# An mLSTM cell with a cosine-gated block behind it: three equal cuts and the scheduler's TensorE order in place of half-height pairs and a written order

## The chip, the cores and the metric

The kernel runs on one core of a Trainium2 chip. A core has a matrix engine (TensorE, PE in the profile, with its weight loads as PEld), three engines that work element by element (VectorE or DVE, ScalarE or ACT, GpSimd or POOL), a queue engine (SyncE or SP), and DMA engines that move data between the large memory and the core's on-chip memory (SBUF). TensorE writes its results to a small accumulator memory, PSUM, which has eight banks; a bank holds 512 f32 columns over 128 partitions. Each engine works through its own list of instructions in order, and engines wait for each other only through semaphores. The metric is the time of one execution in microseconds (us) on the device; lower is better.

## The reference

Two blocks follow each other. The first is an mLSTM cell, run over 768 time steps for 4 batches and 8 heads of size 40:

```
for t in range(S):
    m_new  = max(f[t] + m, i[t])
    f_stab = exp(f[t] + m - m_new);  i_stab = exp(i[t] - m_new);  m = m_new
    C = f_stab * C + i_stab * outer(v[t], k[t])
    n = f_stab * n + i_stab * k[t]
    y[t] = sigmoid(o[t]) * (C @ q[t]) / max(|n . q[t]|, 1)
```

The second block takes each time step's 8 x 40 = 320 numbers as one row x of a matrix of 3072 rows:

```
h = x @ w_in            # 320 -> 2048
out = (h * cos(h)) @ w_out   # 2048 -> 320
```

All is computed in f32. The two weight matrices arrive as 64-bit floats, so the kernel turns their bits into 32-bit floats itself.

## The kernel before

The recurrence is not run step by step. Time is cut into 6 chunks of 128 steps (NC), and a *cell* handles one chunk of one batch, for all 8 heads at once; there are 24 cells. The state that a chunk leaves to the next is kept per batch in `st`.

The gates come first (`gate`): running sums and running maxima of the gate inputs along time give, for each chunk, the columns aT, wT, gT and the running maxima M. M of the first chunk stays on chip as M0; M of the later chunks goes to the large memory, and `load_E` brings it back, spread over 128 partitions, from POOL's queue into a tile E. For the first chunk, eight small matmuls (`pm`, L232) against one column of the identity do that spreading. `decay` then makes each head's 128 x 128 matrix of decays in E: eight DVE instructions (L233) and one exp on ACT (L235). It runs one cell ahead of its use.

A cell then takes these steps. PE transposes q and k (pt, L254), and ACT and DVE copy them out as the tiles t (L256). PE multiplies them into scores (ps, L265), 8 heads in pairs of row groups: the 40 rows of an even head start at partition 0, those of an odd head at partition 64, and the two kinds alternate. DVE multiplies scores and decays (L268). PE computes what the old state gives (pq, L274) and what the chunk itself gives (ph, L280). DVE adds the two and divides (hs, dn, y, L284 to L295), and copies y's last 64 columns once more behind its end (L296). PE transposes y (px, L304), and ACT copies it out as xT (L305). For the next chunk's state, POOL has weighted the keys (kw, L249), PE multiplies them with v (pu, L310), and DVE scales the old state (L320) and adds (L321).

The second block works on a chunk of 4 x 128 = 512 columns. The 2048 hidden features are 16 blocks of 128 (NF). `up` makes two blocks at a time: the 320 rows of w_in are cut into 128 + 128 + 64, the first two cuts are full matmuls (L335), and the 64-row rests of the two blocks are stored on partitions 0 to 63 and 64 to 127 and issued next to each other (L338), which is what y's second copy is for. `act` computes h * cos(h): two ACT passes over the result (n at L345, h at L349), a DVE instruction that takes the rounded turns away (r, written over n, L347), a sine on ACT (L350), and a product on POOL (g, L352). `down` multiplies g with w_out (po, L366) and adds up over the 16 blocks; the four batches have a PSUM bank each, so all four sums grow together, and after the last block ACT copies each out (L369) and SP stores it.

PSUM is divided into 2 banks for the cells (ps_a), 2 for up (ps_u) and 4 for down (ps_o). The four cells of the first chunk run before any up, with the cells taking turns between ps_a and ps_o. After them PE's order is written out by hand (`manual_schedule`): an up pair, a step of the cell of the next chunk, a down of the pair before, the next step, and so on. The order on the other engines, and PE's before that point, is made by a scheduler that plans with estimated times and priorities.

w_in is converted in 10 pieces beside the first four cells, w_out in 16 pieces beside the first chunk's ups. One piece is a DMA from SP's queue into a tile `bits`, two ACT instructions, three on DVE (L124, L126, L128) and an add on POOL (L129); five bits buffers are in use. q, k and v have five buffer sets.

Of the kernel before, what the change touches and what calls it, by code (L numbers as in the profile page):

```python
# [11 lines left out]
FP = mybir.dt.float32  # L12
I32 = mybir.dt.int32
# [15 lines left out]
def kernel(  # L29
# [32 lines left out]

    NK = DM // 128
    KL = NK * 128
    assert DM - KL == 64 and NF % 2 == 0
    NB = 5
# [5 lines left out]
    p4 = ctx.enter_context(tc.tile_pool(name="p4", bufs=4))  # L72
    pb = ctx.enter_context(tc.tile_pool(name="pb", bufs=5))
    dram = ctx.enter_context(tc.tile_pool(name="dram", bufs=1, space=bass.MemoryType.DRAM))
    ps_a = ctx.enter_context(tc.tile_pool(name="ps_a", bufs=2, space=bass.MemoryType.PSUM))
    ps_u = ctx.enter_context(tc.tile_pool(name="ps_u", bufs=2, space=bass.MemoryType.PSUM))
    ps_o = ctx.enter_context(tc.tile_pool(name="ps_o", bufs=4, space=bass.MemoryType.PSUM))
# [23 lines left out]

    w_in_sb = wp.tile([128, NK, DFF], FP, name="w_in_sb")

    w_in_l = wp.tile([128, NF // 2, 128], FP, name="w_in_l")
# [6 lines left out]
    def to_float32(dst, src):  # L111
        rows, n = dst.shape
        r = slice(0, rows)
        bits = pb.tile([128, WP, 2], I32, name="bits", tag="bits")
        for part, piece in src:
            nc.sync.dma_start(out=bits[part, 0:n], in_=piece)
# [14 lines left out]
    def weights_in(f):  # L131
        for i in range(NK):
            to_float32(w_in_sb[:, i, ts(f, WP)], [(slice(0, 128), w_in_bits[ts(i, 128), ts(f, WP)])])

    def weights_in_l(f):
        src = w_in_bits[KL:DM].rearrange("r (a e n) two -> r e a n two", e=2, n=128)
        n = WP // 128
        to_float32(w_in_l[:, ts(f, n)].rearrange("p a n -> p (a n)"),
                   [(slice(64 * e, 64 * e + 64), src[:, e, ts(f, n)]) for e in range(2)])

    def weights_out(f):
        to_float32(w_out_sb[:, f], [(slice(0, 128), w_out_bits[ts(f, 128)])])
# [20 lines left out]
    def gate(c):  # L163
# [13 lines left out]
        pg = ps_o.tile([128, 4, BH], FP, name="pg", tag="o")  # L177
# [14 lines left out]
    gp = ctx.enter_context(tc.tile_pool(name="gp", bufs=8))  # L192
# [19 lines left out]
    def load_E(n):  # L212
        c, b = divmod(n, B)
        E = p4.tile([128, H, C], FP, name="E", tag="E")
        if c > 0:
            src = M_d[b * H:(b + 1) * H, ts(c - 1, C)]
            nc.gpsimd.dma_start(out=E, in_=src.unsqueeze(0).to_broadcast([128, H, C]))  # L217
        loaded[n] = E

    def decay(n):  # L220

        c, b = divmod(n, B)
        E = loaded[n]
        for h in range(H):
            g = b * H + h
            m = E[:, h]
            if c == 0:

                if h % HP == 0:
                    pm = ps_u.tile([128, HP, C], FP, name="pm", tag="up")  # L230
                m = pm[:, h % HP]
                nc.tensor.matmul(m, ident[0:BH, g:g + 1].to_broadcast([BH, 128]), M0, start=True, stop=True)  # L232
            nc.vector.scalar_tensor_tensor(out=E[:, h], in0=m, scalar=aT[:, c, g:g + 1],  # L233
                                           in1=late, op0=OP.subtract, op1=OP.max)
        nc.scalar.activation(out=E, in_=E, func=AF.Exp, scale=-1.0)  # L235

    def cell(n, psum, tag):

# [8 lines left out]
        if c < NC - 1:  # L247
            kw = p2.tile([128, H, 64], FP, name="kw", tag="kw")
            nc.gpsimd.tensor_tensor(out=kw, in0=ks[i], in1=cols(wT, 64), op=OP.mult)  # L249
        tT = []  # L250
        for src, copy in ((qs[i], nc.scalar.copy), (ks[i], nc.vector.tensor_copy)):
            pt = psum.tile([128, HP, C], FP, name="pt", tag=tag)
            for p in range(HP):
                nc.tensor.transpose(pt[:, p], src[:, 2 * p:2 * p + 2].rearrange("p j d -> p (j d)"), ident)  # L254
            t = p2.tile([128, HP, C], FP, name=f"t{len(tT)}", tag=f"t{len(tT)}")
            copy(out=t, in_=pt)  # L256
            tT.append(t)
        qT, kT = tT
        yield

        ps = [psum.tile([128, HP, C], FP, name="ps", tag=tag) for _ in range(2)]
        for p in range(HP):
            for j in range(2):
                r = slice(64 * j, 64 * j + D)
                nc.tensor.matmul(ps[j][:, p], kT[r, p], qT[r, p], start=True, stop=True)  # L265
        for j in range(2):
            w = E.rearrange("p (a j) t -> p a j t", j=2)[:, :, j]
            nc.vector.tensor_tensor(out=w, in0=ps[j], in1=w, op=OP.mult)  # L268
        yield

        if c > 0:
            pq = psum.tile([128, H, D1], FP, name="pq", tag=tag)
# [3 lines left out]
        ph = psum.tile([128, H, D1], FP, name="ph", tag=tag)  # L276
        for j in range(2):
            for p in range(HP):
                h = 2 * p + j
                nc.tensor.matmul(ph[:, h], E[:, h], vs[i][:, h], start=True, stop=True)  # L280
        hs = ph
        if c > 0:
# [9 lines left out]
        y = p2.tile([128, 2 * DM - KL], FP, name="y", tag="y")  # L292
        yh = y[:, 0:DM].rearrange("p (h d) -> p h d", h=H)
        nc.vector.tensor_tensor(out=yh, in0=sig[c][:, b], in1=hs[:, :, 0:D], op=OP.mult)
        nc.vector.tensor_tensor(out=yh, in0=yh, in1=dn.unsqueeze(2).to_broadcast([128, H, D]), op=OP.mult)  # L295
        nc.vector.tensor_copy(out=y[:, DM:], in_=y[:, KL:DM])  # L296
        yield


        if b == 0:  # L300
            xT[c] = p2.tile([128, NK + 1, B, C], FP, name="xT", tag="xT")
        px = psum.tile([128, NK + 1, C], FP, name="px", tag=tag)
        for i2 in range(NK + 1):
            nc.tensor.transpose(px[:, i2], y[:, ts(i2, 128)], ident)  # L304
        nc.scalar.copy(out=xT[c][:, :, b], in_=px)  # L305

        if c < NC - 1:
            pu = psum.tile([128, HP, 2, D1], FP, name="pu", tag=tag)
# [13 lines left out]
        yield  # L322
# [4 lines left out]
    def up(c, f2):  # L327
        pair = [ps_u.tile([128, B * C], FP, name="pup", tag="up") for _ in range(2)]

        def x(i, r=slice(0, 128)):  # L330
            return xT[c][r, i].rearrange("p b t -> p (b t)")

        for e, pu in enumerate(pair):
            for i in range(NK):
                nc.tensor.matmul(pu, w_in_sb[:, i, ts(2 * f2 + e, 128)], x(i), start=(i == 0), stop=False)  # L335
        for e, pu in enumerate(pair):
            r = slice(64 * e, 64 * e + 64)
            nc.tensor.matmul(pu, w_in_l[r, f2], x(NK, r), start=False, stop=True)  # L338
        for e, pu in enumerate(pair):
            act(c, 2 * f2 + e, pu)  # L340

    def act(c, f, pu):

        n = p3.tile([128, B * C], I32, name="n", tag="n")
        nc.scalar.activation(out=n, in_=pu, func=AF.Copy, bias=0.25)  # L345
        r = n.bitcast(FP)
        nc.vector.scalar_tensor_tensor(out=r, in0=pu, scalar=0.25, in1=n, op0=OP.add, op1=OP.subtract)  # L347
        h = p3.tile([128, B * C], FP, name="h", tag="h")
        nc.scalar.activation(out=h, in_=pu, func=AF.Copy, scale=TWO_PI)  # L349
# [5 lines left out]
    po = {}  # L355

    def down(c, f2):
        if f2 == 0:
            po[c] = [ps_o.tile([128, DM], FP, name="po", tag="o") for _ in range(B)]
        last = f2 == NF // 2 - 1  # L360

        order = [(f, b) for f in (2 * f2, 2 * f2 + 1) for b in range(B)]
        if last:
            order.sort(key=lambda fb: fb[1])
        for f, b in order:
            nc.tensor.matmul(po[c][b], gs[c, f][:, ts(b, C)], w_out_sb[:, f], start=(f == 0), stop=(f == NF - 1))  # L366
            if f == NF - 1:
                o = p2.tile([128, DM], FP, name="o_sb", tag="o_sb")
                nc.scalar.copy(out=o, in_=po[c][b])  # L369
                nc.sync.dma_start(out=out[b * S + c * C:b * S + (c + 1) * C], in_=o)  # L370


    N = NC * B

    def ahead(n):

        if n + NB - 1 < N:
            load(n + NB - 1)
        if n + 3 < N:
            load_E(n + 3)  # L380
        if n % B == B - 1 and n + 1 < N:
            gate_o(n // B + 1)

    gates_in()
    load(0)
    for n in range(3):
        load_E(n)
    gate(0)
    for n in range(1, NB - 1):
        load(n)  # L390
    gate_o(0)


    for n in range(B):
        decay(n)
        for _ in cell(n, *((ps_a, "a"), (ps_o, "o"))[n % 2]):
            pass
        ahead(n)
# [4 lines left out]
        weights_in(n)  # L403
        if n % 2 == 1:
            weights_in_l(n // 2)
    decay(B)

    with tc.manual_schedule(engines={mybir.EngineType.PE}):  # L410
        for c in range(NC):
            for b in range(B):
                n = (c + 1) * B + b
                steps = iter(())
                if n < N:
                    steps = cell(n, ps_a, "a")
# [46 lines left out]
```

## Time and profile before

| | |
|---|---|
| median of 3 runs | 684.95 us (684.32 to 685.29) |
| the profiled execution's own time | 685.29 us |
| its span in the profile | 683.5 us |
| mean granted TensorE clock | 0.985 of full speed |
| PE busy | 627.3 us, 2786 records |
| DVE, ACT, POOL busy | 349.4, 305.7, 193.5 us |
| moved by DMA | 41.42 MB, most of it in packets under 512 bytes |

A profile shows one execution. Its groups collect the instructions of one line, engine and shape: busy time, mean length of one, and the idle time of the engine just before them with what ended it. Starts and lengths of single instructions are in its timeline; matmuls overlap in a pipeline, so what a matmul costs is read from the distance between starts, not from its length. The span can be cut into stages, and each engine's busy time read per stage.

### The profile page before, as it was taken

How to read it: one execution, taken by the hardware profiler on the slowest of the kernel's cores; microseconds unless marked ns; L12 is line 12 of the kernel's file. 1: busy time of each engine (PE TensorE's matmuls, PEld its weight loads, DVE VectorE, ACT ScalarE, POOL GpSimd, SP SyncE). 2: the span in 40 equal slices, each digit the busy share in tenths (PEclk: the TensorE clock that was granted, in tenths of full speed). 3: DMA queues.
4: the chain of work that ended last, by engine and by line, in shares of the span. 5: the costliest groups of instructions: out<-in, count | busy, mean ns of one | idle time of the engine just before them, and what ended most of it. 6: DMA issues, size and time to landing. Idle time of an engine off the chain costs nothing.

```text
span 683.5 us, 7830 instructions
## 1 busy us (share of the span) xinstructions
PE 627.3 (92%) x2786; PEld 395.6 (58%) x2786; DVE 349.4 (51%) x752; ACT 305.7 (45%) x498; POOL 193.5 (28%) x190
## 2 busy tenths in 40 slices
PE   4998559969999999999999999999999999999997
PEld 3887535545565565566556556556556566655554
DVE  5467788782663663663573573563563343321110
ACT  2433557744537525527435437434435232334332
POOL 4023245451331331331321321322222212122221
PEclk9999988979999999999999999999999999999999
DMA  9966856511223211223311232211111000000001
GB/s 141 200 121 122 211 145 146 126 41 20 60 57 80 61 34 26 60 62 76 61 41 20 59 72 67 60 42 20 40 32 39 0 1 0 1 24 16 0 1 38
DMA packets 110888, 41.42 MB, mean 61 GB/s; under 512 B 101041, under 2 KB 105137, under 8 KB 110849
## 3 DMA queue, kind: packets, MB, share of 16 engines
q1 hardware_dynamic: 107888, 30.25, 23.0%
q0 software_dynamic: 2912, 10.57, 4.9%
q8 instruction: 22, 0.36, 0.2%
q14 instruction: 18, 0.14, 0.1%
q10 hardware_dynamic: 48, 0.10, 0.0%
HBM read 36.90 MB, written 4.01 MB: 60 GB/s over the span
## 4 chain that ended last, share of the span: by engine, by line
PE 65%; DVE 21%; ACT 9%; issue 3%; DMA 1%; POOLq 0%; POOL 0%; DVEq 0%; ACTq 0%
PE pup L335 24%; PE po L366 11%; PE pup L338 7%; PE ph L280 7%; DVE st L320 7%; PE ps L265 4%; PE pq L274 3%; PE pu L310 3%; ACT L350 2%; ACT h L349 2%; ACT n L350 2%; DVE E L233 2%; PE px L304 2%; DVE n L347 2%; PE pm L232 2%
## 5 line engine op out<-in xcount | busy, mean ns | idle before, releaser
L366 PE MATMUL po<-w_out_sb,g 128*128 128x320 f32 x768 | 217.2, 436 | 0.2 <-POOL g L352 0.2
L352 POOL TENSOR_TENSOR g<-h,n 128x512 f32<-128x512 f32 x96 | 121.2, 1286 | 245.8 <-ACT n L350 239.0
L335 PE MATMUL pup<-xT,w_in_sb 128*128 128x512 f32 x384 | 181.1, 616 | 0.6 <-ACT xT L305 0.6
L366 PEld LDWEIGHTS po<-w_out_sb,g 128*128 128x128 f32 x768 | 142.2, 190 | 59.9 <-issue 6.1
L347 DVE SCALAR_TENSOR_TENSOR n<-pup,n 128x512 f32<-128x512 f32 x96 | 62.1, 686 | 208.2 <-ACT n L345 208.2
L345 ACT ACTIVATE n<-pup 128x512 int32<-128x512 f32 x96 | 52.3, 593 | 173.1 <-PE pup L338 173.1
L335 PEld LDWEIGHTS pup<-xT,w_in_sb 128*128 128x128 f32 x384 | 71.9, 196 | 76.7 <-issue 71.5
L268 DVE TENSOR_TENSOR E<-ps,E 128x512 f32<-128x512 f32 x48 | 30.9, 685 | 71.3 <-PE ps L265 71.2
L349 ACT ACTIVATE h<-pup 128x512 f32<-128x512 f32 x96 | 56.8, 592 | 11.1 <-DVE n L347 11.1
L233 DVE SCALAR_TENSOR_TENSOR E<-E,aT,late 128x128 f32<-128x128 f32 x160 | 60.7, 440 | 0.1
L350 ACT ACTIVATE n<-n 128x512 f32<-128x512 f32 x96 | 60.1, 626 | 0.2
L305 ACT COPY xT<-px 128x384 f32<-128x384 f32 x24 | 11.5, 478 | 107.6 <-PE px L304 107.6
L217 POOL DMA_DIRECT2D E<-M_d x20 | 18.4, 922 | 138.1 <-ACT h L349 67.5
L280 PE MATMUL ph<-vs,E 128*128 128x41 f32 x384 | 53.0, 302 | 2.4 <-DVE E L268 2.4
L338 PE MATMUL pup<-xT,w_in_l 64*128 64x512 f32 x192 | 54.2, 641 | 0.0
L280 PEld LDWEIGHTS ph<-vs,E 128*128 128x128 f32 x384 | 51.6, 215 | 3.2 <-DVE E L268 2.9
L320 DVE TENSOR_TENSOR st<-st,dec 64x164 f32<-64x164 f32 x32 | 49.3, 1541 | 0.5
L265 PE MATMUL ps<-t,t 40*128 40x128 f32 x384 | 34.0, 319 | 9.6 <-DVE t L256 7.6
L265 PEld LDWEIGHTS ps<-t,t 40*128 40x128 f32 x384 | 28.1, 215 | 20.4 <-ACT t L256 8.1
L304 PE MATMUL px<-ident,y 128*128 128x128 f32 x72 | 15.2, 313 | 26.2 <-DVE y L295 25.1
L249 POOL TENSOR_TENSOR kw<-ks,wT 128x512 f32<-128x512 f32 x20 | 21.0, 1050 | 62.1 <-issue 56.1
L338 PEld LDWEIGHTS pup<-xT,w_in_l 64*128 64x128 f32 x192 | 14.5, 184 | 36.4 <-issue 36.4
(75 smaller groups left out, 561.1 us busy)
## 6 DMA issues: line engine op xcount, KB each, us to landing
E<-M_d POOLq DMA_DIRECT2D x20, 512.0 KB, 4.8
bits<-in_moe_w_out_dram SPq DMA_DIRECT2D x16, 320.0 KB, 3.3
bits<-in_moe_w_in_dram SPq DMA_DIRECT2D x8, 512.0 KB, 5.0
qs<-in_q_dram SPq DMA_DIRECT2D x24, 160.0 KB, 3.3
ks<-in_k_dram SPq DMA_DIRECT2D x24, 160.0 KB, 3.6
vs<-in_v_dram SPq DMA_DIRECT2D x24, 160.0 KB, 2.8
o<-in_o_gate_dram SPq DMA_DIRECT2D x24, 160.0 KB, 3.7
out_dram<-o_sb SPq DMA_DIRECT2D x24, 160.0 KB, 1.8
```

Source lines behind the costliest of these rows:

```text
L233: nc.vector.scalar_tensor_tensor(out=E[:, h], in0=m, scalar=aT[:, c, g:g + 1], in1=late, op0=OP.subtract, op1=OP.max)
L265: nc.tensor.matmul(ps[j][:, p], kT[r, p], qT[r, p], start=True, stop=True)
L280: nc.tensor.matmul(ph[:, h], E[:, h], vs[i][:, h], start=True, stop=True)
L320: nc.vector.tensor_tensor(out=s, in0=s, in1=d.unsqueeze(2).to_broadcast([64, HP, D1]), op=OP.mult)
L335: nc.tensor.matmul(pu, w_in_sb[:, i, ts(2 * f2 + e, 128)], x(i), start=(i == 0), stop=False)
L338: nc.tensor.matmul(pu, w_in_l[r, f2], x(NK, r), start=False, stop=True)
L345: nc.scalar.activation(out=n, in_=pu, func=AF.Copy, bias=0.25)
L347: nc.vector.scalar_tensor_tensor(out=r, in0=pu, scalar=0.25, in1=n, op0=OP.add, op1=OP.subtract)
L349: nc.scalar.activation(out=h, in_=pu, func=AF.Copy, scale=TWO_PI)
L350: nc.scalar.activation(out=r, in_=r, func=AF.Sin, scale=TWO_PI_DOWN)
L352: nc.gpsimd.tensor_tensor(out=g, in0=h, in1=r, op=OP.mult)
L366: nc.tensor.matmul(po[c][b], gs[c, f][:, ts(b, C)], w_out_sb[:, f], start=(f == 0), stop=(f == NF - 1))
```

## The change

The other kernel does the same computation with these differences.

- **Cuts.** The 320 rows are cut at head borders into 120, 120 and 80, all from partition 0. `up` makes one block of 128 features at a time with three matmuls; there are no half-height pairs, y is written over the sigmoid tile, and xT is copied out by two ACT copies. w_in has 12 pieces.
- **Scores.** The four even heads go first into a bank of their own, then the four odd heads into another.
- **Order.** The order by hand is gone; the scheduler places all of PE's work. The cell is one function without steps, with the decays inside it, the weighted keys (kw) behind y, and pq behind ph. `down` takes one batch at a time over all 16 blocks, after the chunk's ups in the source.
- **Buffers.** PSUM: 3 banks for the cells, 2 for the scores, 2 for up, 1 for down. 19 buffers for g (8 before), 3 for E (4), 3 for bits (5), 4 sets for q, k and v (5). E is loaded two cells ahead (three before).
- **Early stage.** w_in's pieces are issued ahead of each of the first four cells; the cells use the same three banks.

```diff
-    NK = DM // 128
-    KL = NK * 128
-    NB = 5
+    KH = 3
+    cuts = [(h * D, min(h + KH, H) * D) for h in range(0, H, KH)]
+    KD = KH * D
+    full = DM // KD
+    NK = len(cuts)
+    NB = 4
...
-    p4 = ctx.enter_context(tc.tile_pool(name="p4", bufs=4))
-    pb = ctx.enter_context(tc.tile_pool(name="pb", bufs=5))
-    ps_a = ctx.enter_context(tc.tile_pool(name="ps_a", bufs=2, space=bass.MemoryType.PSUM))
+    ps_a = ctx.enter_context(tc.tile_pool(name="ps_a", bufs=3, space=bass.MemoryType.PSUM))
+    ps_s = ctx.enter_context(tc.tile_pool(name="ps_s", bufs=1, space=bass.MemoryType.PSUM))
...
-    ps_o = ctx.enter_context(tc.tile_pool(name="ps_o", bufs=4, space=bass.MemoryType.PSUM))
+    ps_o = ctx.enter_context(tc.tile_pool(name="ps_o", bufs=1, space=bass.MemoryType.PSUM))
...
-        bits = pb.tile([128, WP, 2], I32, name="bits", tag="bits")
+        bits = p3.tile([128, WP, 2], I32, name="bits", tag="bits")
...
     def weights_in(f):
-        for i in range(NK):
-            to_float32(w_in_sb[:, i, ts(f, WP)], [(slice(0, 128), w_in_bits[ts(i, 128), ts(f, WP)])])
+        for i, (lo, hi) in enumerate(cuts):
+            to_float32(w_in_sb[0:hi - lo, i, ts(f, WP)], w_in_bits[lo:hi, ts(f, WP)], nc.sync)
...
-    gp = ctx.enter_context(tc.tile_pool(name="gp", bufs=8))
+    gp = ctx.enter_context(tc.tile_pool(name="gp", bufs=19))
...
-        E = p4.tile([128, H, C], FP, name="E", tag="E")
+        E = p3.tile([128, H, C], FP, name="E", tag="E")
...
-        ps = [psum.tile([128, HP, C], FP, name="ps", tag=tag) for _ in range(2)]
-        for p in range(HP):
-            for j in range(2):
-                r = slice(64 * j, 64 * j + D)
-                nc.tensor.matmul(ps[j][:, p], kT[r, p], qT[r, p], start=True, stop=True)
         for j in range(2):
+            r = slice(64 * j, 64 * j + D)
+            ps = ps_s.tile([128, HP, C], FP, name=f"ps{j}", tag=f"s{j}")
+            for p in range(HP):
+                nc.tensor.matmul(ps[:, p], kT[r, p], qT[r, p], start=True, stop=True)
...
-        y = p2.tile([128, 2 * DM - KL], FP, name="y", tag="y")
...
-        nc.vector.tensor_copy(out=y[:, DM:], in_=y[:, KL:DM])
+        y = sig[c][:, b]
...
         if c < NC - 1:
+            kw = p2.tile([128, H, 64], FP, name="kw", tag="kw")
+            nc.gpsimd.tensor_tensor(out=kw, in0=ks[i], in1=cols(wT, 64), op=OP.mult)
...
-    def up(c, f2):
-        pair = [ps_u.tile([128, B * C], FP, name="pup", tag="up") for _ in range(2)]
...
-        for e, pu in enumerate(pair):
-            for i in range(NK):
-                nc.tensor.matmul(pu, w_in_sb[:, i, ts(2 * f2 + e, 128)], x(i), start=(i == 0), stop=False)
-        for e, pu in enumerate(pair):
-            r = slice(64 * e, 64 * e + 64)
-            nc.tensor.matmul(pu, w_in_l[r, f2], x(NK, r), start=False, stop=True)
...
+    def up(c, f):
+        pu = ps_u.tile([128, B * C], FP, name="pup", tag="up")
+        for i, (lo, hi) in enumerate(cuts):
+            r = slice(0, hi - lo)
+            nc.tensor.matmul(pu, w_in_sb[r, i, ts(f, 128)], xT[c][r, i].rearrange("p b t -> p (b t)"),
+                             start=(i == 0), stop=(i == NK - 1))
...
+    def down(c, b):
+        po = ps_o.tile([128, DM], FP, name="po", tag="o")
+        for f in range(NF):
+            nc.tensor.matmul(po, gs[c, f][:, ts(b, C)], w_out_sb[:, f], start=(f == 0), stop=(f == NF - 1))
+        o = p2.tile([128, DM], FP, name="o_sb", tag="o_sb")
+        nc.scalar.copy(out=o, in_=po)
+        nc.sync.dma_start(out=out[b * S + c * C:b * S + (c + 1) * C], in_=o)
...
-    with tc.manual_schedule(engines={mybir.EngineType.PE}):
...
+    for c in range(NC):
+        for b in range(B):
+            for f in range(b * NF // B, (b + 1) * NF // B):
+                up(c, f)
+                if c == 0:
+                    weights_out(f)
+            if c + 1 < NC:
+                step((c + 1) * B + b)
+        for b in range(B):
+            down(c, b)
```

## The prediction

> **What bounds the kernel now.** I read the page's busy table and chain first, then a table of six stages of my own cut (one for each chunk of 128 time steps), then the groups that the change touches, and at last the timeline of single instructions, because a group's mean hides how matmuls overlap.
>
> ```profile
> PE 627.3 (92%) x2786; PEld 395.6 (58%) x2786; DVE 349.4 (51%) x752; ACT 305.7 (45%) x498; POOL 193.5 (28%) x190
> ...
> PE 65%; DVE 21%; ACT 9%; issue 3%; DMA 1%; POOLq 0%; POOL 0%; DVEq 0%; ACTq 0%
> ...
> L335 PE MATMUL pup<-xT,w_in_sb 128*128 128x512 f32 x384 | 181.1, 616 | 0.6 <-ACT xT L305 0.6
> L338 PE MATMUL pup<-xT,w_in_l 64*128 64x512 f32 x192 | 54.2, 641 | 0.0
> L265 PE MATMUL ps<-t,t 40*128 40x128 f32 x384 | 34.0, 319 | 9.6 <-DVE t L256 7.6
> L304 PE MATMUL px<-ident,y 128*128 128x128 f32 x72 | 15.2, 313 | 26.2 <-DVE y L295 25.1
> ```
>
> TensorE (PE) is the bound: 92% busy, and its idle time has one large cause, px waiting for y (25.1 us). The stages, whose columns are length, then busy time of PE, its weight loads, DVE, ACT and POOL, the granted clock and DMA, say where PE is full. The first line starts at the first up pair, the second at the second pair:
>
> ```profile
> 85.90:102.56 16.66, 9.56 (x38) 5.06 (x37) 15.23 (x30) 9.54 (x17) 8.15 (x8) 0.81 0.58 142
> 102.56:203.62 101.06, 90.80 (x411) 56.27 (x409) 68.19 (x139) 53.87 (x91) 38.41 (x36) 0.93 0.32 74
> 203.62:305.72 102.10, 97.03 (x462) 60.21 (x462) 55.75 (x109) 48.22 (x75) 27.84 (x24) 1.00 0.25 53
> 509.70:603.04 93.34, 92.60 (x430) 56.77 (x428) 35.04 (x66) 34.37 (x63) 21.25 (x16) 1.00 0.02 8
> 603.04:683.50 80.46, 76.81 (x240) 41.11 (x240) 10.31 (x16) 28.85 (x56) 19.97 (x16) 1.00 0.05 17
> ```
>
> In a steady chunk (third line) PE idles 5.1 of 102.1 us, so PE work that is added there is paid nearly in full. Prices come from starts in PE's timeline and, for y's wait, from DVE and POOL beside it (columns: start, length):
>
> ```profile
> 589.11 1.16 PE L265 MATMUL ps<-t,t 40*128 40x128 f32 x16
> 590.20 3.70 PE L335 MATMUL pup<-xT,w_in_sb 128*128 128x512 f32 x8
> ...
> 612.14 3.60 PE L335 MATMUL pup<-xT,w_in_sb 128*128 128x512 f32 x8
> 615.66 1.13 PE L338 MATMUL pup<-xT,w_in_l 64*128 64x512 f32 x4
> 616.72 4.57 PE L366 MATMUL po<-w_out_sb,g 128*128 128x320 f32 x16
> ...
> 350.12 3.38 DVE L320 TENSOR_TENSOR st<-st,dec 64x164 f32<-64x164 f32 x1
> 374.67 0.31 DVE L320 TENSOR_TENSOR st<-st,dec 64x164 f32<-64x164 f32 x1
> ...
> 350.80 2.50 POOL L352 TENSOR_TENSOR g<-h,n 128x512 f32<-128x512 f32 x2
> ...
> 355.08 0.52 PE L304 MATMUL px<-ident,y 128*128 128x128 f32 x3 [1.14 <-DVE y L295]
> ```
>
> Every f32 matmul shows as two records, or passes. Eight 512-column passes take 615.66 - 612.14 = 3.52, 0.44 each. Four half-height passes take 616.72 - 615.66 = 1.06, not 4 x 0.44 = 1.76: the halves on rows 0-63 and 64-127 overlap.
>
> **The change, part by part.**
>
> *Up projection.* A pair of feature blocks costs 3.52 + 1.06 = 4.58 now. Afterwards each block has three cuts of 120, 120 and 80 rows, all starting at row 0, so nothing is paired: 12 passes of 0.44 = 5.28. 48 pairs x 0.70 = +33.6 us, on PE. Bounds: passes of 128 and 64 rows have the same mean (616 and 641 ns), so fewer rows buy nothing; that the 80-row cut scales with its rows (80/128) would take 96 x 0.88 x 0.375 = 31.7 off. I take +33.6.
> The Trainium skill (TensorEngine Tiling, Theoretical Speedup) puts two-way row tiling at up to 2x. By that the pair of halves would be 0.88, and the loss 0.88 per pair, 42 us; the row above gives 1.06 and 33.6, and the measurement decides.
>
> *Scores (ps).* Now the two row groups alternate, 16 passes in 590.20 - 589.11 = 1.09. Afterwards four products of one group precede four of the other. Neighbours that do not pair: ph, 16 passes in 1.75 (595.84 to 597.59 in the same timeline), and pt, four passes in 0.49, so 1.96 for 16. I take 1.80, nearest to ph, for +0.71; ends +0.66 and +0.87, and 0 if order did not matter. Twenty cells after the first up: +14.2.
>
> *Order and waits.* The fixed order px, up pair, pt, po, ps, up pair, pq, ph, po goes; the scheduler's order of the built program has, in each steady cell, ps, one ph, pq, half of pu, the other ph, half of pu, three up matmuls, px, eight up matmuls, pt, three po, one up. Before px, PE now has half of pu (0.43) and three ups (3 x 0.88 = 2.64) after ph, 3.1 us. On DVE from ph to y: hs add 0.42, two state adds 0.65, then dn, y, dn, reciprocal, y 1.44 (353.53 to 354.97), 2.5 in all; the state decays now stand ahead of the hs add, beside ph. So y is just covered. In the steady chunks PE idles 5.07, 4.67, 5.09 and 0.74 us now (stage length less busy), 15.6 in all; I leave it about 1 us a chunk and take -11. Lower end: all gone, -15.6. Upper end: the decay on DVE took 3.38 while POOL worked through an E issue and two g products and 0.31 when it did not; if a block of up to 3.1 lands between ph and y in each of 16 cells, PE pays 3.1 - 0.6 = 2.5 a cell, +40.
> The Trainium skill (SBUF — State Buffer, shared port pair) calls this an exclusive lock held for a whole instruction, with the loser fully blocked. The 3.38 against 0.31 agrees; since the new order spreads the g products singly instead of two together, the rule lets a block recur at more places, which speaks against the change and for the upper end.
> kw moves after y in the source, but POOL still issues it cells ahead of pu; nobody waits. The decays of E move into the cell: PE does not wait for them while po and pt (2.6 us) stand before ps. E is fetched two cells ahead instead of three, from POOL's queue, and lands in 4.8 us against a cell of about 19; covered twice over. q, k, v come four cells ahead into four buffers behind out stores on SP; a whole chunk of slack. The dropped y copy (L296, 236 ns on DVE) and a second xT copy on ACT are off the path, and 19 g buffers in place of 8 hold a chunk's 16 blocks and three of the next.
>
> *Down projection.* Same 384 matmuls, 0.55 each (616.72 to 621.13 is 4.41 for eight). With one PSUM bank, each of the 24 sums must be copied out before the next starts. The nearest row is the up pair at 603.04, which waited 0.57 for ACT to copy xT out; the copy of a sum is no longer (0.428 against 0.478 mean). In the new order one up matmul (0.88) covers that gap within five chunks; only in the last one three gaps are bare: 3 x 0.6 = +1.8. If the fifteen covers fail, 9 more.
>
> *Up to the second up pair (102.56 us now).* Weight pieces go from 10 to 12 (L129 on POOL 1.31 each, DVE 1.85 a piece by L124, L126, L128). PE takes the first four cells strictly one after another, where two of them interleave now. PE is not the limit here (9.56 of the last 16.66). Each cell is a chain at PE's early pace (from its timeline there): pt 1.9, eight decays and exp 3.5, unpaired scores about 4, two products 1.3, ph and pu 5.5, y 2, px and its copy 1, together 19, and 2 of DVE's weight work between. The first ends near 32, since sigmoid now ends at 31.4 on ACT; three more make 95; of the first ups the seventh matmul needs the first block's r, which DVE reaches after some 9 us of weights and decays: I get 105 for the same progress. +3, between -8 (interleaving hidden anyway) and +25 (three bits buffers instead of five make SP's queue hold loads behind weights).
> *First chunk.* 10.3 idle now, DVE at 68 of 101. w_out's 16 pieces stay in it or just before: 0, between -8 and +12.
>
> **Sum.** 33.6 + 14.2 - 11 + 1.8 + 3 = +41.6. The profiled execution took 685.29 with a span of 683.5, 1.8 outside; 683.5 + 41.6 + 1.8 = 726.9. The median of the runs, 684.95, lies 0.3 lower: 727.
>
> **Rivals.**
> *DVE's chain becomes the wait (slower still).* POOL's blocks fall between ph and y in all 16 cells: +40 instead of -11, 778; in half of them, 758. For it: 3.38 in nearly every cell now, and 6.51 us of wait for y at 141.9 in the first chunk. Against: the decays stand earlier in the new order.
> *The stage before the ups grows.* +25 instead of +3: 749. For it: fewer buffers and one cell at a time at a granted clock of 0.81. Against: PE has slack.
> *Not slower: the early stage speeds up.* PE is busy 75 of the first 102.56 us (sum over 17-us windows), much of it slowly: ps takes 2.0 there, 1.09 later. If the new order ran it densely at full speed, that work is near 45 us. It decides if the second pair starts before 102.6 - 38.6 = 64 us; at 58 the time would be 727 - 47.6 = 679. Against: PE there waits for DVE, whose own work there is 66 us now (same windows) and does not shrink.
> *The order does not matter to ps, and waits vanish wholly.* 0 instead of 14.2 and -15.6: 708.
>
> **How the numbers follow.** My sum within 15 us (712 to 742): 52%. DVE's chain: 20% (742 to 780). Early stage longer: 13% (735 to 760). Waits vanish: 10% (698 to 712). Faster: 4%; within 0.2%, about what a measurement of this kernel can tell: 1%; slower 95%. The range 702 to 762 leaves out the faster case, the bottom of the fourth and the top of the second, some 15%.
>
> **What would show it.** Up: 576 records, PE start to start 0.44, no pairs. ps: near 1.8 for 16 passes. px's wait for y: a few us in all; if it is 30 or more, DVE's chain was the step that failed. po's wait for the copy only in the last three sums. The first up near 96 us, the steady chunk near 105. A ps that still takes 1.1, or a first up before 70, would make the forecast wrong.

## The result, and the profile after

| | before | after |
|---|---|---|
| median of 4 runs each | 684.92 us (684.32 to 685.29) | 747.72 us (745.29 to 750.87) |
| ratio | | 1.092, 95% interval 1.0866 to 1.0975 |
| the profiled execution, its span | 685.29 us, 683.5 us | 745.29 us, 743.4 us |

The change costs 62.8 us; 42 were forecast. The time lies in the predicted range, 20.7 us above the number. Below, `after_raw` and `after_three` are given without one execution each that was over 1.5% above the fastest of its kernel. The same views as before, now of the changed kernel: the page's busy table, chain and the groups of up, scores and px.

```profile
PE 675.4 (91%) x2786; PEld 435.7 (59%) x2786; DVE 321.0 (43%) x734; ACT 317.7 (43%) x529; POOL 196.1 (26%) x189
...
PE 69%; DVE 13%; DMA 10%; issue 3%; SPq 2%; ACT 2%; POOL 0%; ACTq 0%; DVEq 0%; POOLq 0%
...
L310 PE MATMUL pup<-xT,w_in_sb 120*128 120x512 f32 (+1 forms) x576 | 271.2, 611 | 10.5 <-DVE n L318 10.5
L239 DVE SCALAR_TENSOR_TENSOR E<-E,aT,late 128x128 f32<-128x128 f32 x160 | 62.8, 451 | 23.5 <-DMA E<-M_d 23.4
L247 PE MATMUL ps<-t,t 40*128 40x128 f32 x384 | 50.1, 313 | 0.4 <-ACT t L226 0.3
L297 PE MATMUL px<-ident,o 128*120 128x128 f32 (+1 forms) x72 | 14.1, 311 | 21.0 <-DVE o L271 19.3
```

PE stays the bound. Two things are new: up (L310) now waits for r on DVE (L318), and DVE's decays (L239) wait 23.4 us for the DMA that brings E. px still waits 21.0 us in all (26.2 before), although only a few us of it were to stay. The chain holds 10% DMA; it held 1%.

The stages of the changed kernel, with the same columns as before (length, busy PE, PEld, DVE, ACT, POOL, granted clock, DMA share, GB/s). The second line shown starts where the third block of 128 features begins, the same progress as the second pair before:

```profile
0.00:106.12 106.12, 73.56 (x300) 62.23 (x301) 68.15 (x195) 41.63 (x73) 32.98 (x50) 1.00 0.75 134
...
113.43:225.77 112.34, 102.71 (x447) 64.78 (x447) 62.48 (x132) 59.81 (x96) 36.41 (x33) 0.98 0.31 68
225.77:337.47 111.70, 104.98 (x463) 66.55 (x462) 50.04 (x105) 51.87 (x82) 29.52 (x25) 1.00 0.23 49
...
557.37:664.40 107.03, 104.67 (x429) 65.84 (x428) 30.00 (x64) 35.92 (x67) 21.20 (x17) 0.95 0.04 12
664.40:743.40 79.00, 74.12 (x219) 40.92 (x217) 10.37 (x15) 27.85 (x50) 19.01 (x15) 1.00 0.03 11
```

The difference of the spans, 743.4 - 683.5 = 59.9, splits without a rest. The same progress is reached at 113.43 instead of 102.56: +10.9. From there to the end it is 629.97 instead of 580.94 us: PE's busy time grew by 43.1 and its idle time by 5.9 (35.4 against 29.5). The clock is no part of this difference: behind that point the kernel before had 0.93 over 101.06 us, the changed one 0.98 over 112.34 and 0.95 over 107.03, some 7 us of full clock lost in each. A steady chunk takes 111.70 us (102.10 before), with PE idle for 6.7.

### The profile page after: what moved, and what is told of

Its sections match the earlier page's. It is cut to its first block, busy times and chain, and to the rows that moved or that the text cites. A ratio compares the mean times of both kernels' runs of the same rounds, so it can differ in the third digit from the quotient of the medians.

```text
span 743.4 us, 7889 instructions
## 1 busy us (share of the span) xinstructions
PE 675.4 (91%) x2786; PEld 435.7 (59%) x2786; DVE 321.0 (43%) x734; ACT 317.7 (43%) x529; POOL 196.1 (26%) x189
## 4 chain that ended last, share of the span: by engine, by line
PE 69%; DVE 13%; DMA 10%; issue 3%; SPq 2%; ACT 2%; POOL 0%; ACTq 0%; DVEq 0%; POOLq 0%
PE po L327 27%; PE pup L310 22%; DMA E<-M_d 8%; PE ph L253 7%; DVE E L239 5%; PE ps L247 4%; PE pt L224 3%; PE pq L258 2%; PE pu L278 2%; DVE E L249 2%; DMA bits<-in_moe_w_in_dram 2%; SPq L201 2%; PE pm L238 1%; DVE n L318 1%; PE px L297 1%
## 5 line engine op out<-in xcount | busy, mean ns | idle before, releaser
L310 PE MATMUL pup<-xT,w_in_sb 120*128 120x512 f32 (+1 forms) x576 | 271.2, 611 | 10.5 <-DVE n L318 10.5
L310 PEld LDWEIGHTS pup<-xT,w_in_sb 120*128 120x128 f32 (+1 forms) x576 | 106.5, 194 | 128.3 <-issue 95.4
L318 DVE SCALAR_TENSOR_TENSOR n<-pup,n 128x512 f32<-128x512 f32 x96 | 65.0, 686 | 211.0 <-ACT h L316 210.5
L239 DVE SCALAR_TENSOR_TENSOR E<-E,aT,late 128x128 f32<-128x128 f32 x160 | 62.8, 451 | 23.5 <-DMA E<-M_d 23.4
L329 ACT COPY o_sb<-po 128x320 f32<-128x320 f32 x24 | 10.2, 425 | 138.5 <-PE po L327 121.7
L247 PEld LDWEIGHTS ps<-t,t 40*128 40x128 f32 x384 | 42.9, 209 | 17.0 <-ACT n L319 5.9
L247 PE MATMUL ps<-t,t 40*128 40x128 f32 x384 | 50.1, 313 | 0.4 <-ACT t L226 0.3
L226 DVE COPY t<-pt 128x512 f32<-128x512 f32 x24 | 16.6, 690 | 44.7 <-PE pt L224 44.4
L241 ACT ACTIVATE E<-E 128x1024 f32<-128x1024 f32 x24 | 25.3, 1055 | 21.9 <-DVE E L239 21.9
L297 PE MATMUL px<-ident,o 128*120 128x128 f32 (+1 forms) x72 | 14.1, 311 | 21.0 <-DVE o L271 19.3
L118 ACT ACTIVATE wm<-bits 128x320 int32<-128x320 uint32 (+2 forms) x28 | 15.9, 566 | 37.5 <-POOL w_in_sb L126 15.5
L298 ACT COPY xT<-px 120x256 f32<-120x256 f32 x24 | 8.8, 367 | 49.1 <-PE px L297 49.0
```

What stands on the lines that cost most here:

```text
L247: nc.tensor.matmul(ps[:, p], kT[r, p], qT[r, p], start=True, stop=True)
L310: nc.tensor.matmul(pu, w_in_sb[r, i, ts(f, 128)], xT[c][r, i].rearrange("p b t -> p (b t)"), start=(i == 0), stop=(i == NK - 1))
```

## The experiments

Seven kernels start from the changed one and undo one thing (or three), five start from the kernel before and do one thing. Ratios are to the kernel before, which was run again beside each. The changed kernel was not; its 747.72 stands for it, and `after_gp17`, which differs from it by two buffers, had 747.70.

### Steady chunks: is it E's landing that holds up DVE's queue?

The timeline of one steady cell of the changed kernel (columns: start, length, and in brackets the idle time before it):

```profile
373.37 0.49 DVE L262 TENSOR_TENSOR hs<-hs,ph 128x328 f32<-128x328 f32 x1 [0.89 <-PE ph L253]
373.63 0.92 POOL L208 DMA_DIRECT2D E<-M_d  x1 [3.44 <-PE ph L253]
374.09 1.57 DVE L266 TENSOR_SCALAR dn<-hs 128x8 f32<-128x8 f32 x1
374.58 1.06 POOL L275 TENSOR_TENSOR kw<-ks,wT 128x512 f32<-128x512 f32 x1
377.41 0.52 PE L297 MATMUL px<-ident,o 128*120 128x128 f32 x3 [0.97 <-DVE o L271]
378.63 3.20 DVE L239 SCALAR_TENSOR_TENSOR E<-E,aT,late 128x128 f32<-128x128 f32 x8 [0.64 <-DMA E<-M_d]
381.75 0.68 DVE L318 SCALAR_TENSOR_TENSOR n<-pup,n 128x512 f32<-128x512 f32 x1
382.48 2.84 PE L310 MATMUL pup<-xT,w_in_sb 120*128 120x512 f32 x6 [0.26 <-DVE n L318]
```

With three E buffers, POOL can refill one only when ph has read it (373.63, after a wait of 3.44 for ph). The scheduler puts the eight decays on that fresh E at once into DVE's list. DVE works in order, so it stands until the DMA lands at 378.63, takes 3.20 for the decays, and only then makes r (L318), for which up waits. The same POOL burst starts right behind ph and falls on dn, which takes 1.57 instead of 0.16: px waits 0.97.

`after_raw` takes the reason for the wait away: the DMA fills a tile of its own, of two buffers, and the decays go from it into E. To make room, g has 17 buffers; `after_gp17` has that alone.

```diff
+            raw = p2.tile([128, H, C], FP, name="Mb", tag="Mb")
-            nc.gpsimd.dma_start(out=E, in_=src...)
+            nc.gpsimd.dma_start(out=raw, in_=src...)
...
+        E = p2.tile([128, H, C], FP, name="E", tag="E")
-            m = E[:, h]
+            m = raw[:, h] if c > 0 else None
```

> The changed kernel with the spread maxima read into a tile of their own (2 buffers) and the decays written into E (2 buffers); g has 17 buffers instead of 19 to make room. So the load's buffer is freed by the decays and no longer by ph of a cell. Theory: in the changed kernel the load waits for ph, then the decays sit in DVE's queue waiting for the load to land, ahead of r, and POOL's issue of the load beside kw holds up the dn instruction; so px's wait for y (0.97 in most cells) and up's wait for r (0.26 to 1.16) shrink by 12 to 20 us, to 728 to 736. Rival: the waits come from the g products and the length of DVE's chain whatever the load does: 747 within 4.

> The changed kernel with 17 buffers for g instead of 19, as a control for the run with the load's own tile. Both theories: 747 within 4, since 16 hold a chunk and only the first block of the next chunk is made during the sums of the last.

`after_raw`: 738.69 us (728.91 to 738.84), ratio 1.0736 (1.0661 to 1.0811). `after_gp17`: 747.70 us, ratio 1.0905 (1.0865 to 1.0945), the same as the changed kernel. The median fell by 9, between the two expectations. The times of `after_raw` follow the granted clock: 728.91 us at 0.991, 738.84 in the profiled execution at 0.972, and the changed kernel's 745.29 us also came at 0.991, so at like clock it is 16. Two whole chunks each, from one first score to the next, show it without the clock's part (first the changed kernel, then `after_raw`):

```profile
236.29:347.12 110.83, 104.12 (x460) 66.20 (x461) 49.45 (x105) 49.14 (x78) 28.43 (x25) 1.00 0.22 48
347.12:457.65 110.53, 104.13 (x461) 66.22 (x461) 48.77 (x105) 49.14 (x78) 28.41 (x24) 1.00 0.23 49
```

```profile
251.41:357.35 105.94, 103.98 (x462) 66.88 (x462) 43.42 (x105) 50.13 (x79) 28.56 (x25) 1.00 0.25 51
357.35:463.27 105.92, 103.11 (x460) 65.85 (x459) 43.11 (x104) 48.77 (x78) 28.44 (x25) 1.00 0.23 50
```

PE's busy time stays within 1 us, and its idle time falls from 6.6 to 2.4 a chunk. In the trace the up group's wait for r falls from 10.5 to 1.7 us, px's for DVE from 19.3 to 12.8. In the second of the two chunks px's waits were 3.84 us and up's 1.62; `after_raw` has 1.23 and none. So the run shows that these waits hang on when E's buffer comes free, at 4.8 us a chunk. It changes three things at once and doesn't part them: the decays wait for no DMA, r moves in among them, and POOL issues the load later, away from dn, which takes 0.92 in place of 1.57. Why its clock was lower (0.81 to 0.86 between 107 and 230 us) is not shown.

Up's wait for r does not need the landing, as `after_ps_alt` (under Scores) shows, where E's buffers are those of the changed kernel:

```profile
349.92 3.21 DVE L239 SCALAR_TENSOR_TENSOR E<-E,aT,late 128x128 f32<-128x128 f32 x8 [0.17 <-DMA E<-M_d]
353.05 0.68 DVE L320 SCALAR_TENSOR_TENSOR n<-pup,n 128x512 f32<-128x512 f32 x1
353.79 2.84 PE L312 MATMUL pup<-xT,w_in_sb 120*128 120x512 f32 x6 [1.14 <-DVE n L320]
```

The decays wait only 7.3 us for the DMA in that run, but up waits 14.1 for r: eight decays of 3.2 us ahead of r in DVE's list are enough.

### Up: what are the unpaired cuts worth?

`before_up_split` does what the change does to the pairs: each block's 64-row rest follows its own two cuts.

```diff
         for e, pu in enumerate(pair):
             for i in range(NK):
                 nc.tensor.matmul(pu, w_in_sb[:, i, ts(2 * f2 + e, 128)], x(i), start=(i == 0), stop=False)
-        for e, pu in enumerate(pair):
             r = slice(64 * e, 64 * e + 64)
```

> The kernel before with one edit: each feature block's 64-row matmul follows its own two full ones, so the two halves of a pair are no longer neighbours; nothing else moves. If the half-height pair's overlap is what the three equal cuts give up, the time rises by 48 x 0.70 = 33.6 us to about 718 (715 to 721). If TensorE's idle time absorbs it (29.5 us idle after the second pair), the rise stays below 10, at most 695. In the profile the 64-row passes would go from a start distance of 0.27 on average to 0.44.

715.30 us (714.99 to 715.70), ratio 1.0441 (1.0424 to 1.0458): +30.3, as the theory had it, but not for its reason. From its PE timeline in the last chunk:

```profile
634.10 1.88 PE L335 MATMUL pup<-xT,w_in_sb 128*128 128x512 f32 x4
635.91 1.12 PE L337 MATMUL pup<-xT,w_in_l 64*128 64x512 f32 x2
636.97 1.98 PE L335 MATMUL pup<-xT,w_in_sb 128*128 128x512 f32 x4
638.88 1.12 PE L337 MATMUL pup<-xT,w_in_l 64*128 64x512 f32 x2
639.93 4.57 PE L365 MATMUL po<-w_out_sb,g 128*128 128x320 f32 x16
```

A lone half-height rest takes 1.06 us for two passes (636.97 - 635.91), as much as two paired rests take for four, and more than two full passes (0.88). A pair is 639.93 - 634.10 = 5.83, 1.25 more than before, which is 60 us over 48 pairs. PE's busy time did grow by 55 (682.4 against 627.3), and its idle time fell by 25 (31.3 against 56.2): the slower up covers y, and px's wait fell from 26.2 to 4.9. The run therefore doesn't price the changed kernel's cuts. Their price is read in the changed kernel itself, where 90 passes of 120 and 80 rows run on end:

```profile
664.40 38.86 PE L310 MATMUL pup<-xT,w_in_sb 120*128 120x512 f32 x90
703.10 8.78 PE L327 MATMUL po<-w_out_sb,g 128*128 128x320 f32 x32
712.39 8.88 PE L327 MATMUL po<-w_out_sb,g 128*128 128x320 f32 x32 [0.52 <-ACT o_sb L329]
```

(703.10 - 664.40) / 90 = 0.43 a pass, 5.16 for a pair's 12 passes against 4.58: +0.58 to +0.70 a pair, 28 to 34 us. The 80-row cut is no cheaper (604 ns mean against 614).

`after_pair` gives the changed kernel the old cuts and pairs back:

```diff
-    def up(c, f):
-        pu = ps_u.tile([128, B * C], FP, name="pup", tag="up")
+    def up(c, f2):
+        pair = [ps_u.tile([128, B * C], FP, name="pup", tag="up") for _ in range(2)]
...
+        for e, pu in enumerate(pair):
+            r = slice(64 * e, 64 * e + 64)
+            nc.tensor.matmul(pu, w_in_l[r, f2], x(NK, r), start=False, stop=True)
```

> The changed kernel with the old cuts of the up projection alone (128, 128 and 64 rows, the two 64-row halves of a pair next to each other, on rows 0-63 and 64-127). Theory (the unpaired cuts cost PE 48 x 0.6 to 0.7 us, and nothing else takes it up): 747.7 - 29 to 34, so 714 to 719 us, with a pair at 4.6 in the trace. Rival (PE's longer work covered waits, as when the halves were separated in the kernel before: PE's busy time grew by 55 us there, its idle time fell by 25, and the time by 30 only): px and the up projection wait longer for DVE here, more than 15 us is given back, and the time is 730 or more.

803.59 us (801.47 to 805.25), ratio 1.173 (1.1703 to 1.1758): 56 us slower, where the theory had 29 to 34 faster. The rival holds, far beyond what it named. From its PE timeline:

```profile
392.96 0.70 PE L340 MATMUL po<-w_out_sb,g 128*128 128x320 f32 x2
396.08 5.40 PE L318 MATMUL pup<-xT,w_in_sb 128*128 128x512 f32 x8 [2.41 <-DVE n L331]
401.40 1.13 PE L321 MATMUL pup<-xT,w_in_l 64*128 64x512 f32 x4
```

A pair takes both banks of up at once, and the next pair needs both free; in this order only pt and one po stand between these two pairs (392.03 to 393.66), so PE waits for ACT and DVE to empty them (30.3 us before up, 22.2 before ph). E's landing has a part in it: DVE's decays wait 48.1 us for the DMA here (23.4 in the changed kernel), and in this cell r came behind them:

```profile
393.76 1.66 DVE L244 SCALAR_TENSOR_TENSOR E<-E,aT,late 128x128 f32<-128x128 f32 x6 [3.33 <-DMA E<-M_d]
395.34 0.68 DVE L331 SCALAR_TENSOR_TENSOR n<-pup,n 128x512 f32<-128x512 f32 x1
```

And the pause costs twice: the eight passes behind it take 401.40 - 396.08 = 5.32, not 3.52, at a granted clock of 0.68. The mean clock is 0.917 over 800.9 us, up to 66 us of full clock lost against 7 in the changed kernel; by this estimate it is the larger part of the loss. PE's idle time is 26 us longer. The Trainium skill (TensorE: Matmul & The Clock Gate, What's actually happening) says that PE's clock is throttled by default and only sustained activity releases it; the rows agree in kind. So the old cuts alone are no remedy in this order. That pairs need the written order, with a block of po between two pairs, is argued and not shown: no run has pairs with a tile of its own for the load.

### Scores

`before_ps_grouped` and `after_ps_alt` swap the two loops, in the kernel before (even heads first; its diff is shown) and in the changed one (alternating again).

```diff
-        for p in range(HP):
-            for j in range(2):
+        for j in range(2):
+            for p in range(HP):
                 r = slice(64 * j, 64 * j + D)
                 nc.tensor.matmul(ps[j][:, p], kT[r, p], qT[r, p], start=True, stop=True)
```

> The kernel before with one edit: the four even heads' scores are issued first, then the four odd ones. Theory: neighbours in different row groups overlap, grouped ones don't; the changed kernel's trace has 1.68 us for 16 grouped passes against 1.09 alternating, so 20 to 24 cells x 0.59 = +12 to +14 us, 697 to 699. Rival: the order of the scores does not reach the end, since DVE's product or the waits after it set the pace: 685 within 2.

> The changed kernel with the score products alternating between the two row groups again, all else as it is. Theory: 16 passes take 1.1 instead of 1.7 to 1.8 us, 16 cells in the steady part and 4 early: 747.7 - 10 to 14, so 733 to 738 us. Rival (the scores stand where PE has slack, or DVE's products of the first group start later and take it back): 744 us or more.

`before_ps_grouped`: 702.81 us (702.58 to 703.11), ratio 1.026 (1.0244 to 1.0275), +17.8. The two parts of its time:

```profile
0.00:91.66 91.66, 71.69 (x294) 60.33 (x295) 52.30 (x172) 31.38 (x49) 23.15 (x44) 1.00 0.81 149
91.66:700.80 609.14, 570.83 (x2493) 350.78 (x2492) 296.13 (x580) 273.70 (x450) 169.52 (x146) 0.99 0.19 46
```

Behind the first up it is 609.14 instead of 597.60: +11.5, or 0.58 for each of the 20 cells there, where 0.71 was forecast; the scores themselves take 1.64 instead of 1.09. The rest is the early stage, +5.8, where the first cell's scores alone take 3.02 instead of 2.01. The rival falls; the theory, +12 to +14 in all, counted the early cells no dearer than the others.

`after_ps_alt`: 724.88 us (723.51 to 727.26), ratio 1.0594 (1.0566 to 1.0623): 22.8 gained, beyond both expectations. ps accounts for 14.3 (the group falls from 50.1 to 35.8). PE's idle time is 5.8 lower: the scheduler now puts four up matmuls ahead of px in most steady cells instead of three, and px's wait falls from 21.0 to 12.5. Work and order can't be changed apart where a scheduler decides.

### The early stage: which part takes the 11 us?

Four runs, each one difference. `before_serial` runs the first four cells in ps_a alone; `before_bits3` has three landing buffers.

```diff
-        for _ in cell(n, *((ps_a, "a"), (ps_o, "o"))[n % 2]):
+        for _ in cell(n, ps_a, "a"):
```

> The kernel before with its first four cells in one pair of PSUM banks, so that two of them no longer interleave; the rest as it is. If cells one after another are what made the early stage long: second up pair near 111 instead of 102.6, and 692 to 697 us. If interleaving is hidden by DVE's weight work: 684 to 687 us.

> The kernel before with three landing buffers for the weights instead of five; nothing else. If the smaller landing ring is what made the early stage of the changed kernel longer: first up pair 10 us or more later than 85.9, and 693 us or more. If it is the rest (the order of DVE's, ACT's and POOL's work): first up within 3 us of 85.9, and 683 to 688 us.

`before_serial`: 684.36 us, ratio 0.9991 (0.9980 to 1.0002). `before_bits3`: 683.37 us, ratio 0.9986 (0.9969 to 1.0003). In the kernel before, neither matters: interleaving is hidden, and three landing buffers are enough.

`after_wlast` issues each weight block behind the cell of its number:

```diff
-        if n < NW:
-            weights_in(n)
         if n < B:
             step(n)
+        if n < NW:
+            weights_in(n)
```

> The changed kernel with each weight block of the up projection issued behind the cell of the same number instead of ahead of it; nothing else. Theory (weights ahead of cells cost the early stage: the first px stood behind ACT's work on a piece that landed at 26.6 us, behind 17 us of load issues): first up matmul near 96 instead of 106.1, and 737 to 741 us. Rival (the early stage is long because four cells run one after another on PE and DVE): first up at 104 to 107, and 745 to 750 us.

754.71 us (751.95 to 761.06), ratio 1.1031 (1.0977 to 1.1086): 7.0 slower, the first up at 111.63 instead of 106.12. Both expectations miss; weights ahead of the cells help.

`after_pmu` puts the first chunk's stabilizers, pm, into up's two banks, which stand empty then:

```diff
-                    pm = ps_a.tile([128, HP, C], FP, name="pm", tag="a")
+                    pm = ps_u.tile([128, HP, C], FP, name="pm", tag="up")
```

> The changed kernel with the first chunk's stabilizers (pm) in the two banks of the up projection, which are free then, instead of in the three banks that the cells' other products share. If the ring of three banks holds the first four cells back: cells 18 us apart instead of 22 to 30, first up at 92 to 98 instead of 106.1, and 735 to 741 us. If not: first up at 103 to 108, and 744 to 750 us.

736.34 us (734.76 to 742.48), ratio 1.0769 (1.0715 to 1.0822): 11.4 gained. The last px of the four cells and the first up, from PE's timeline, of the changed kernel and then of `after_pmu`:

```profile
104.16 0.89 PE L297 MATMUL px<-ident,o 128*120 128x128 f32 x3 [1.83 <-DVE o L271]
...
106.12 10.19 PE L310 MATMUL pup<-xT,w_in_sb 120*128 120x512 f32 x18
```

```profile
29.50 6.15 PE L238 MATMUL pm<-M,ident 32*128 32x128 f32 x20 [0.44 <-DVE E L239]
36.09 0.79 PE L238 MATMUL pm<-M,ident 32*128 32x128 f32 x2 [0.44 <-DVE E L239]
...
95.02 0.86 PE L297 MATMUL px<-ident,o 128*120 128x128 f32 x3 [1.06 <-DVE o L271]
96.95 6.32 PE L310 MATMUL pup<-xT,w_in_sb 120*128 120x512 f32 x12
```

With banks of its own, pm runs 20 passes on end for the next cells before the first px; in the changed kernel pm shares three banks with pt, ph, pu and px and comes piecemeal between the scores. The kernel before had pm in up's banks. The first up stands at 96.95, where the prediction had put it (near 96).

### Together

`after_three` undoes three: alternating scores, raw stabilizers, pm in up's banks.

> The changed kernel with three things undone together: scores alternating, the raw stabilizers in a tile of their own (two buffers, E in two, 17 g buffers), the first chunk's pm in the up projection's banks. If the three causes are separate, their single gains add: 747.7 - 22.8 - 9 to 16 - 11.4, so 697 to 705 us, the first up near 97, and what is left above the kernel before is the price of the unpaired cuts less the waits that it covers. If they share one idle time (px's and the up projection's waits for DVE): 710 us or more.

715.77 us (711.13 to 718.92), ratio 1.0432 (1.0390 to 1.0474): 32.0 gained, where the single gains add to 43 (22.8 + 9.0 + 11.4) or more. The rival holds. Its steady chunk:

```profile
335.41:443.25 107.84, 102.20 (x461) 63.79 (x461) 45.51 (x105) 47.98 (x78) 28.95 (x25) 1.00 0.23 51
```

PE is busy for 102.2 and idle for 5.6 again: px waits 1.34 in the chunk's last cell, the first full sum of po 2.12 for ACT to copy its predecessor out, and up 0.60 for r in each of three cells, where r stands behind the decays again, now without a DMA. So waits that one edit took away come back, or others come up, when the order changes with the next edit. Which of them would go next was not tried.

### A kernel faster than both

The kernel before loses px's 1.14 us per cell to a like cause: the second state decay on DVE takes 3.38 us while POOL issues E and works on two g products. `before_hs_stpool` moves the decay to POOL, and keeps hs in ph's PSUM bank.

```diff
-            nc.vector.tensor_tensor(out=hs, in0=hs, in1=ph, op=OP.add)
+            nc.vector.tensor_tensor(out=ph, in0=h0, in1=ph, op=OP.add)
...
-                    nc.vector.tensor_tensor(out=s, in0=s, in1=d..., op=OP.mult)
+                    nc.gpsimd.tensor_tensor(out=s, in0=s, in1=d..., op=OP.mult)
```

> The kernel before with the state's decay (L320) done by POOL instead of DVE, and the sum hs written into the PSUM bank of ph, so that DVE's chain from ph to y reads PSUM. Theory (px waits 1.14 us in nearly every steady cell because the second state decay on DVE is held for 3.4 us while POOL issues E and works on two g products): the wait goes in some 16 cells, px's wait falls from 25 us to under 8, and the time is 665 to 672 us. Rival (another operation of the chain is held in its place, or POOL's longer queue makes g late for the down projection): 682 us or more.

666.23 us (666.03 to 666.95), ratio 0.9722 (0.9707 to 0.9736): 2.8% faster than before. The same place in a steady cell, and a stretch of 97 us in its steady chunks:

```profile
339.87 0.92 POOL L217 DMA_DIRECT2D E<-M_d  x1 [0.98 <-ACT h L349]
340.15 0.17 DVE L289 TENSOR_SCALAR dn<-ph 128x8 f32<-128x8 f32 x1
340.87 2.74 POOL L352 TENSOR_TENSOR g<-h,n 128x512 f32<-128x512 f32 x2
341.06 1.42 DVE L295 TENSOR_TENSOR y<-y,dn 128x320 f32<-128x320 f32 x1
342.51 1.14 DVE L296 COPY y<-y 128x64 f32<-128x64 f32 x1
343.79 0.49 PE L304 MATMUL px<-ident,y 128*128 128x128 f32 x3
```

```profile
275.00:372.00 97.00, 96.50 (x462) 60.73 (x461) 49.39 (x102) 48.34 (x75) 32.65 (x32) 1.00 0.26 56
```

px no longer waits in any steady cell. dn, which now reads PSUM, takes 0.17 beside POOL's issue; y (L295) and its copy (L296), which read SBUF alone, now stretch from 0.49 and 0.19 to 1.42 and 1.14 beside g, but end at 343.65, just ahead of PE. The state's decay takes 0.46 on POOL where it took 1.54 in the mean on DVE. The two edits were not run apart.

## Why the prediction was right, and where it was not

Sign, range and bound were right: PE is full, and work added to it was paid. The number was not: 747.7 lies outside its own band of 712 to 742, and the range holds it because it took in the rivals.

| term | forecast | what the runs show |
|---|---|---|
| up, unpaired cuts | +33.6 | +28 to +34 from the changed kernel's own rows |
| scores grouped, 20 cells | +14.2 | +11.5 behind the first up in the kernel before |
| waits in the steady chunks | -11 | PE's idle time there +5.4 (15.6 to 20.9), +5.9 to the end |
| down's one bank | +1.8 | 0.52 + 0.52 + 0.56 = 1.6, the three bare gaps |
| up to the second pair | +3 | +10.9 |
| clock | none | none: some 7 us lost in both profiled executions |

**Up.** The size holds, and so does it that fewer rows buy nothing. The Trainium skill (TensorEngine Tiling (Array Packing), Theoretical Speedup) puts two-way row tiling at up to 2x. The prediction set that against full-height passes and found the row short of it; against a lone 64-row rest, which takes 1.06 itself, the pair of rests in 1.06 is just that factor of two. The changed kernel loses less than that factor: its 80-row cuts run at the price of full ones, so a pair of blocks takes 5.16, against 5.83 with lone rests.

**Scores.** "1.80, nearest to ph" was a little high: 16 passes take 1.64 to 1.71, and 20 cells cost 0.58 each instead of 0.71. For the early cells the prediction took "about 4"; the first takes 3.02.

**Waits: the step that failed.** "So y is just covered" and "E is fetched two cells ahead instead of three ... covered twice over" are both wrong. The sum counted when E is asked for, not when a buffer is free to be filled: with three buffers POOL waits for ph, and the landing, with 3.2 us of decays, falls into DVE's queue ahead of r. And dn was priced undisturbed, although POOL's block of DVE stood in the same paragraph as an upper end. "The steady chunk near 105" is short of the prediction's own terms: 97.0 + 8 x 0.70 + 4 x 0.71 = 105.5 for PE alone, 106.5 with 1 idle. PE was busy for 104.1, and the chunk is 110.7 because PE idles 6.6 there, not 1: in the second chunk shown px waits 3.84, up 1.62 and ph 0.92. `after_raw` has the chunk at 105.9. px's wait was to be a few us in all and is 21.0; the rival "DVE's chain becomes the wait" named the kind, but looked at px alone, where it set 30 as its mark, and did not see up's wait for r. The time lies where this rival in its mild form and a longer early stage meet.

**Early stage.** The chain of steps was priced well (first up at 96), but not the three banks that pm now shares: `after_pmu` brings 96.95. The upper bound of the forecast had named the landing buffers instead, which `before_bits3` shows to be harmless in the kernel before.

**Down** and its three bare gaps went as forecast.

## What to carry to other kernels

When a change takes buffers away, ask of each load not how early it is issued but which read frees its buffer, and what stands behind the first user of the data on that user's in-order queue. Here the scheduler put that user ahead of r, and r waited for the DMA and for the user itself.

Price a matmul form from rows of the kernel that uses it, and run it in its own surroundings: separating the halves in the kernel before gave the right total from two errors that cancel (PE +55, waits -25), and putting the pairs back into the changed kernel cost 56 us instead of saving 30. Gains measured singly (43) did not add (32): waits come up again in another place when the order changes.

When a short DVE instruction takes microseconds, look at POOL's line beside it: moving one DVE operation to POOL and one operand to PSUM made this kernel 2.8% faster.

## What the runs showed of the hardware

- Two f32 passes of a 64-row matmul alone take 1.06 us, the same as four passes of two such matmuls on opposite row halves; two passes of 80 to 128 rows take 0.86 to 0.88.
- In `after_pair`, eight passes behind pauses of 2.0 to 3.0 us before up ran at a granted clock of 0.68 to 0.72 (four times; 5.32 us instead of 3.52 behind 2.41). Behind pauses of up to 1.7 us it was 1.00, but for one of 1.47 at 112 us with 0.68. The mean clock was 0.917.
- DVE's eight-column dn, reading SBUF, took up to 1.59 us in the changed kernel beside POOL's E issue and product (median 1.17 over 20). In the kernel before, also from SBUF but mostly away from POOL's work, its median was 0.17, with one of 3.18. In `before_hs_stpool`, where it read PSUM, it took 0.15 to 0.17 in all 24 cases, beside POOL's issue too. The Trainium skill (SBUF — State Buffer, the shared port pair) describes an exclusive lock between DVE and POOL that is held for a whole instruction. That dn is hit from SBUF and spared from PSUM agrees with it, but the run that changed its source also moved it among POOL's work.
- The granted clock of the changed kernel and its variants differed between executions (0.972 to 0.995, `after_pair` aside), with about 10 us between 0.991 and 0.972 in `after_raw`; the kernel before held 0.985 to 0.989. What sets it is open.
